# The last 64 rows of w_down on 64 partitions in place of 128, in a decode layer on one core

## The chip, the core and the metric

The kernel runs on one core of one Trainium2 chip. A core has five engines that take instructions in parallel (TensorE or PE, VectorE or DVE, ScalarE or ACT, GpSimd or POOL, and SyncE or SP) and 16 DMA engines. The metric is the device time of one execution in microseconds (us); lower is better.

## The reference

One token goes through one transformer layer: attention with a cached K and V, then a gated feed-forward block. Everything is bf16.

```
h  = x + attention(layernorm(x), k_cache, v_cache) @ wo      # x is 1 x 640; 32 heads, 4096 keys, 128 wide
n  = layernorm(h)
g, u = n @ w_gate, n @ w_up                                  # 640 x 1728 each
h2 = h + (gelu(g) * u) @ w_down                              # 1728 x 640
```

The two caches have 33.6 MB each, wq and wo 5.2 MB each, w_gate, w_up and w_down 2.2 MB each. Each byte is used once.

## The kernel before, in words

**Loads.** SBUF holds three big slots. The K and V caches come in four groups of eight heads, one transfer for each, and pass through the slots in turn; slot 2 also holds wq first and the feed-forward weights at the end. SP issues nearly all transfers on one queue, in the order of the code. A load waits until the last reader of its slot is done. The feed-forward weights wait for the last use of the third K block (`done[("K", 3)]`), and come in this order: the last 64 rows of w_down (80 KB, line 449), w_gate, w_up in two pieces, then the rest of w_down: rows 0 to 1535 in three pieces (line 453: 1280 KB, 480 KB and 160 KB) and rows 1536 to 1663 in two column pieces (line 454: 64 KB and 96 KB).

**Set-up.** GpSimd builds small masks and selection matrices, some in scratch space of slot 2; VectorE reduces some of them. The second K block is loaded over that scratch space, so its load (in line 429) waits for `free2` (line 300), which lists the query projection `qd` and the last readers of the masks. Two of these are for the change: `c_par` (lines 249 and 263) makes `par`, 1 on even partitions in its first column and on odd ones in its second, and `c_sel2` (line 254) makes `sel2`, a 64 x 128 matrix that spreads 64 values over 128 partitions, each to two neighbours.

**Attention.** For each group VectorE multiplies K by the query (line 312), TensorE and VectorE sum the products (lines 29, 320 and 329), ScalarE takes the exponentials, and TensorE multiplies by V (line 355). The output projection with wo follows (lines 397 to 402).

**Feed-forward.** `glu` (line 488) multiplies the normalized h by w_gate and w_up into rows of PSUM; `turn` (line 499) turns each row into 14 columns, so that value f = 128 m + p of the last two blocks, and similar for the others, stands on a partition; the gelu is worked out in a few VectorE and ScalarE steps (lines 525 to 534). The result is `hm`, 128 x 14 in bf16. Column 13 holds the last 64 values, on partitions 0 to 63; its other half is zero.

**The last projection.** `down` (line 536) runs over blocks m of w_down and over four column ranges q (cut at 0, 128, 256, 448 and 640). For each it loads a column of `hm` as weights and streams the block's columns, accumulating in one PSUM row of `ps_d` for each q. Block 13 is special: its 64 rows of 640 were loaded as 128 half rows of 320, two partitions for each row (line 449). So its weights must stand on 128 partitions: `hp` (line 551) spreads column 13 of `hm` with a matmul by `sel2`, and `h2` (line 553) multiplies the result by `par` into `hm2`, whose two columns are for the left and the right halves. Block 13 then has five matmuls, since the range 256 to 448 crosses the middle at 320; it goes first, in line 554. Blocks 0 to 7, 8 to 10, 11 and 12 follow in lines 555 to 560, each behind its own transfer. VectorE and ScalarE copy the four results out (lines 563 and 565), and SP stores them.

Of the kernel before, what the change touches and what calls it, by code (L numbers as in the profile page):

```python
# [5 lines left out]
FP32 = mybir.dt.float32  # L6
BF16 = mybir.dt.bfloat16
ALU = mybir.AluOpType
ACTF = mybir.ActivationFunctionType
AX = mybir.AxisListType  # L10
# [100 lines left out]
def bass_sequential_preLN__gqa_block_cached__glu_gated_geglu__decode_kernel(nc, A_x, A_k_cache, A_v_cache, A_wq, A_wo, B_x, B_w_gate, B_w_up, B_w_down, out):  # L111
    sb = lambda name, shape, dt: nc.alloc_sbuf_tensor(name, shape, dt)
# [32 lines left out]
    e_t = sb("e_t", [128, 14], FP32)  # L145
    gu = sb("gu", [128, 14], FP32)
    hm = sb("hm", [128, 14], BF16)
    hm2 = sb("hm2", [128, 2], BF16)
    sel2 = sb("sel2", [64, 64, 2], BF16)
    par = sb("par", [128, 2], FP32)  # L150
    one_bf = sb("one_bf", [1, 1], BF16)
    one_f = sb("one_f", [128, 1], FP32)
    mean_f = sb("mean_f", [128, 128], FP32)
# [16 lines left out]
    first_t = Cut(slots[2], 5 * 4096)  # L170
    ones_b = first_t.take(128)
    m4_t = first_t.take(128).rearrange("p (a b) -> p a b", a=4)
    hs_t = first_t.take(128).rearrange("p (a b c) -> p a b c", a=8, b=4)
    m8_t = first_t.take(128).rearrange("p (a b) -> p a b", a=8)
    par_t = first_t.take(128).rearrange("p (a b) -> p a b", a=2)
    x_row = first_t.take(D, 1)
    last_t = Cut(slots[1], 0)
    A_hi, A_lo = last_t.take(D), last_t.take(D)
# [10 lines left out]
    ps_d = bank[4][:, 264:456]  # L189
    ps_s = bank[5]  # L190
    ps_z = bank[6]
# [7 lines left out]
    wd_sb = slots[2][:, 10 * DF:10 * DF + 14 * D].rearrange("p (m n) -> p m n", m=14)  # L199

    P = Prog(nc)
    V = lambda fn, *d: P.op("vector", fn, *d)
    A = lambda fn, *d: P.op("scalar", fn, *d)
    T = lambda fn, *d: P.op("tensor", fn, *d)
# [32 lines left out]
    def mask(dst, src, pattern, base, cm, op, *deps):  # L237
        return GP(lambda e: e.affine_select(dst, src, pattern=pattern, compare_op=op, fill=0.0, base=base,
                                            channel_multiplier=cm), *deps)
    c_idb = mask(id_b[:, :], ones_b[:, 0:128], [[1, 128]], 0, -1, ALU.is_equal, c_onesb)  # L240
# [4 lines left out]
    c_m4 = mask(m4_t, ones_b[:, 0:128].rearrange("p (a b) -> p a b", a=4), [[-1, 4], [-4, 32]], 0, 1, ALU.is_equal)  # L245
    c_hs = mask(hs_t, ones_b[:, 0:128].rearrange("p (a b c) -> p a b c", a=8, b=4), [[-4, 8], [-32, 4], [-1, 4]], 0, 1,
                ALU.is_equal)
    c_s4 = mask(sel4[:, :], ones_b[:, 0:4], [[-32, 4]], 0, 1, ALU.is_equal)
    c_par = mask(par_t, ones_b[:, 0:128].rearrange("p (a b) -> p a b", a=2), [[-1, 2], [-2, 64]], 0, 1, ALU.is_equal)
    c_hx = mask(hbx[:, :, :], ones_b[:, 0:32].rearrange("p (a b) -> p a b", a=8), [[-16, 8], [0, 4]], 0, 1, ALU.is_ge)  # L250
    c_hx = mask(hbx[:, :, :], hbx[:, :, :], [[16, 8], [0, 4]], 15, -1, ALU.is_ge, c_hx)
    c_sel = mask(sel[:, :, :], ones_b[0:16, 0:128].rearrange("p (a b) -> p a b", a=16), [[1, 16], [0, 8]], 0, -1, ALU.is_equal)
    c_m8 = mask(m8_t, ones_b[:, 0:128].rearrange("p (a b) -> p a b", a=8), [[-1, 8], [-8, 16]], 0, 1, ALU.is_equal)
    c_sel2 = mask(sel2[:, :, :], ones_b[0:64, 0:128].rearrange("p (a b) -> p a b", a=64), [[1, 64], [0, 2]], 0, -1,
                  ALU.is_equal)

    c_odd = V(lambda e: e.reduce_sum(odd[:, :], hb[:, 8:16].rearrange("p (a b) -> p b a", b=2), axis=AX.X), c_hb)
    c_far = V(lambda e: e.tensor_scalar(far[:, :, :], odd[:, :].unsqueeze(2).to_broadcast([128, 2, 16]), -1e38, 1e38, ALU.mult, ALU.add), c_odd)
    c_m4 = V(lambda e: e.reduce_sum(m4[:, :], m4_t, axis=AX.X), c_m4)
    c_m8 = V(lambda e: e.reduce_sum(m8[:, :], m8_t, axis=AX.X), c_m8)  # L260
    c_hs = V(lambda e: e.reduce_sum(hs[:, 8:16], hs_t.rearrange("p a b c -> p a (b c)"), axis=AX.X), c_hs, c_hz)
    c_o4 = V(lambda e: e.reduce_max(ones4[:, :], sel4[:, :], axis=AX.X), c_s4)
    c_par = V(lambda e: e.reduce_sum(par[:, :], par_t, axis=AX.X), c_par)


    def x_cols(e):
# [30 lines left out]
        return i  # L297
    qd = T(q_proj, xl, d_wq)
    q1 = V(lambda e: e.tensor_copy(qb[:, :, :].rearrange("p g d -> p (g d)"), ps_q[:, :]), qd)  # L299
    free2 = [qd, c_sel2, c_par, c_m4, c_m8, c_hs, c_idb]  # L300

    folds, reds, exps, pbs, pvs, mks, evs, hds, nbs = {}, {}, {}, {}, {}, {}, {}, {}, {}
    z4s, spr, aPs = {}, {}, {}
# [103 lines left out]
    for G in range(NG):  # L407
# [32 lines left out]
        if G == 2:  # L440
# [5 lines left out]
    free = done[("K", 3)]  # L446
    wu_v = B_w_up[:, :].rearrange("(p c) n -> p c n", c=5)
    wd_v = B_w_down[0:1536, :].rearrange("(p r) n -> p r n", r=12)
    d_wd = [P.dma("sync", wd_sb[:, 13, 0:320], B_w_down[1664:1728, :].rearrange("f (s n) -> (f s) n", s=2), free)]
    d_wg = P.dma("sync", wg_sb, B_w_gate[:, :].rearrange("(p c) n -> p c n", c=5))  # L450
    d_wu = [P.dma("sync", wu_sb[:, 0:3, :], wu_v[:, 0:3, :]),
            P.dma("sync", wu_sb[:, 3:5, :], wu_v[:, 3:5, :])]
# [12 lines left out]
    hi = [V(lambda e: e.tensor_copy(A_hi[0:97, 0:320], bank[0][0:97, 0:320]), pr),  # L465
          A(lambda e: e.copy(A_hi[0:97, 320:640], bank[1][0:97, 0:320]), pr)]
    lo = [V(lambda e, t=t: e.tensor_sub(A_lo[0:97, 320 * t:320 * t + 320], bank[t][0:97, 0:320], A_hi[0:97, 320 * t:320 * t + 320]),
            hi[t]) for t in range(2)]
# [65 lines left out]
    g9 = V(lambda e: e.tensor_mul(hm[:, :], gu[:, :], ps_u[:, 0:14]), g6, up)  # L534

    def down(ms, qs=range(4)):
        def fn(e):
            for m in ms:
                for q in qs:
                    lo, hi = CUT[q], CUT[q + 1]  # L540
                    if m < 13:
                        parts = [(hm[:, m:m + 1], lo, hi, 0)]
                    else:
                        parts = [(hm2[:, s:s + 1], max(lo, 320 * s), min(hi, 320 * s + 320), 320 * s) for s in range(2)]
                    for w, a, b, base in parts:
                        if a < b:
                            i = e.matmul(ps_d[32 * q:32 * q + 1, a - lo:b - lo], w, wd_sb[:, m, a - base:b - base],  # L547
                                         start=False, stop=(m == 12), skip_group_check=(m == 13))
            return i
        return fn  # L550
    hp = T(lambda e: e.matmul(ps_z[:, 0:1], sel2[:, :, :].rearrange("p a b -> p (a b)"), hm[0:64, 13:14],
                              start=True, stop=True), g9, c_sel2)
    h2 = V(lambda e: e.tensor_mul(hm2[:, :], par[:, :], ps_z[:, 0:1].to_broadcast([128, 2])), hp)
    T(down([13]), h2, d_wd[0])
    T(down(range(8)), d_wd[1])
    T(down(range(8, 11)), d_wd[2])
    T(down([11]), d_wd[3])
# [40 lines left out]
```

## Time and profile before

| | |
|---|---|
| three runs, median | 202.17 us (201.92 to 202.38) |
| the profiled execution, its own time | 201.75 us |
| its span, first to last instruction | 200.5 us |
| granted TensorE clock, mean | 0.901 |
| PE, busy | 107.0 us (53%), 771 matmuls |
| PE weight loads, busy | 17.3 us (9%), 490 loads |
| DVE, busy | 118.5 us (59%), 160 instructions |
| ACT, busy | 6.7 us (3%) |
| POOL, busy | 4.2 us (2%) |
| DMA | 84.32 MB in 2890 packets, mean 421 GB/s |

The profile is of one execution, whose span starts at its first instruction; all times within it count from there. The page gives the busy time of each engine, then the span in 40 slices of equal length with the busy share of each in tenths, then the DMA queues, then the chain of waits: from the last instruction back to whatever released each step. Groups of instructions carry the line of the kernel, the engine, the operation, and the tiles they write and read. "PEld" is a weight load on TensorE, "SPq" a DMA issue by SP. A wait for several things is put down to the one that came last by the trace.

### The profile page before, as it was taken

How to read it: one execution, taken by the hardware profiler on the slowest of the kernel's cores; microseconds unless marked ns; L12 is line 12 of the kernel's file. 1: busy time of each engine (PE TensorE's matmuls, PEld its weight loads, DVE VectorE, ACT ScalarE, POOL GpSimd, SP SyncE). 2: the span in 40 equal slices, each digit the busy share in tenths (PEclk: the TensorE clock that was granted, in tenths of full speed). 3: DMA queues.
4: the chain of work that ended last, by engine and by line, in shares of the span. 5: the costliest groups of instructions: out<-in, count | busy, mean ns of one | idle time of the engine just before them, and what ended most of it. 6: DMA issues, size and time to landing. Idle time of an engine off the chain costs nothing.

```text
span 200.5 us, 1514 instructions
## 1 busy us (share of the span) xinstructions
PE 107.0 (53%) x771; PEld 17.3 (9%) x490; DVE 118.5 (59%) x160; ACT 6.7 (3%) x18; POOL 4.2 (2%) x19
## 2 busy tenths in 40 slices
PE   0108000586674408476745095855086897475584
PEld 0103000000001100000022000000000020231232
DVE  3300100889975027999750569997879969624331
ACT  2100000000001000000010000000100000100111
POOL 7100000000000000000000000000000000000000
PEclk9999999999996976999978759999859999979758
DMA  9999999999999999999999999999999998999993
GB/s 360 417 466 431 418 418 418 418 418 510 484 445 431 397 418 431 431 418 431 418 418 422 431 484 458 445 431 418 431 418 431 431 431 368 429 425 425 407 413 121
DMA packets 2890, 84.32 MB, mean 421 GB/s; under 512 B 322, under 2 KB 836, under 8 KB 1092
## 3 DMA queue, kind: packets, MB, share of 16 engines
q1 hardware_dynamic: 2882, 84.23, 97.9%
q8 instruction: 5, 0.08, 0.2%
q14 instruction: 1, 0.01, 0.0%
q10 hardware_dynamic: 2, 0.00, 0.0%
HBM read 84.23 MB, written 0.00 MB: 420 GB/s over the span
## 4 chain that ended last, share of the span: by engine, by line
DMA 52%; DVE 30%; PE 15%; SPq 1%; issue 1%; ACT 0%
DMA slot<-in_A_k_cache_dram 39%; DVE slot L312 21%; DMA slot<-in_B_w_down_dram 12%; PE bank L29 9%; DVE sc L329 6%; PE bank L355 4%; SPq L60 1%; DVE mix L343 1%; PE bank L320 1%; PE bank L547 1%; DVE mx L334 0%; ACT p_t L339 0%; DVE mix L361 0%; DVE mxd L335 0%; DVE mxd L337 0%
## 5 line engine op out<-in xcount | busy, mean ns | idle before, releaser
L312 DVE TENSOR_TENSOR slot<-slot,qb 128x4096 bf16<-128x4096 bf16 x32 | 72.6, 2280 | 32.9 <-DMA slot<-in_A_k_cache_dram 32.9
L29 PE MATMUL bank<-slot,id_b 128*128 128x512 bf16 x249 | 66.0, 417 | 27.2 <-DVE slot L312 27.2
L329 DVE TENSOR_REDUCE sc<-bank 128x32 f32<-128x512 f32 x32 | 21.9, 683 | 11.6 <-PE bank L29 11.6
L355 PE MATMUL bank<-slot,mix 128*32 128x512 bf16 x256 | 19.3, 468 | 8.8 <-DVE mix L343 8.8
L320 PE MATMUL bank<-slot,id_b 128*128 128x512 bf16 x7 | 3.4, 483 | 34.2 <-DVE slot L312 34.2
L355 PEld LDWEIGHTS bank<-slot,mix 128*32 128x32 bf16 x256 | 7.8, 115 | 76.5 <-DVE mix L343 42.1
L295 PE MATMUL bank<-slot,xlnM 128*32 128x512 bf16 x40 | 4.5, 631 | 7.1 <-DMA slot<-in_A_wq_dram 7.1
L339 ACT ACTIVATE p_t<-sc,nb 128x256 bf16<-128x256 f32 x4 | 2.0, 508 | 161.0 <-DVE nb L338 161.0
L343 DVE TENSOR_TENSOR mix<-p_t,hbx 128x512 bf16<-128x512 bf16 x16 | 5.7, 420 | 2.7 <-ACT p_t L339 2.7
L299 DVE CAST qb<-bank 128x512 bf16<-128x512 f32 x1 | 0.7, 691 | 10.1 <-PE bank L295 10.1
L494 PE MATMUL bank<-slot,hlnT 128*1 128x512 bf16 (+1 forms) x40 | 4.8, 552 | 2.1 <-DVE hlnT L482 1.5
L361 DVE TENSOR_TENSOR mix<-bank,m 128x512 f32<-128x512 f32 x4 | 2.7, 682 | 4.4 <-PE bank L355 4.4
L268 PE MATMUL bank<-one_bf,slot 1*128 1x1 bf16 x5 | 0.4, 177 | 7.0 <-DMA slot<-in_A_x_dram 7.0
L320 PEld LDWEIGHTS bank<-slot,id_b 128*128 128x128 bf16 x7 | 0.7, 99 | 37.2 <-DVE slot L312 36.8
L369 PEld LDWEIGHTS bank<-po_r,hb 128*16 128x16 f32 x8 | 0.5, 95 | 31.5 <-issue 31.5
L400 PE MATMUL bank<-slot,aP 128*1 128x320 bf16 x32 | 2.5, 298 | 1.0 <-DMA slot<-in_A_wo_dram 1.0
L29 PE MATMUL bank<-slot,aP 128*1 128x320 bf16 x32 | 2.5, 298 | 0.0
L295 PEld LDWEIGHTS bank<-slot,xlnM 128*32 128x32 bf16 x40 | 1.6, 141 | 9.2 <-issue 9.2
L547 PE MATMUL bank<-slot,hm 128*1 128x128 bf16 (+2 forms) x57 | 2.1, 233 | 0.6 <-DMA slot<-in_B_w_down_dram 0.4
L371 PE MATMUL bank<-po_r,hs 128*16 128x128 f32 x8 | 1.5, 274 | 1.0 <-DVE po_r L365 1.0
L563 DVE CAST slot<-bank 1x128 bf16<-1x128 f32 (+1 forms) x2 | 0.6, 316 | 2.3 <-PE bank L547 2.3
L515 PE MATMUL bank<-mix,one_f 128*1 128x128 f32 (+1 forms) x8 | 2.0, 460 | 0.0
(91 smaller groups left out, 40.6 us busy)
## 6 DMA issues: line engine op xcount, KB each, us to landing
slot<-in_A_wq_dram SPq DMA_DIRECT2D x1, 5120.0 KB, 15.4
slot<-in_A_wo_dram SPq DMA_DIRECT2D x2, 2560.0 KB, 15.9
slot<-in_B_w_gate_dram SPq DMA_DIRECT2D x1, 2160.0 KB, 17.4
slot<-in_B_w_up_dram SPq DMA_DIRECT2D x1, 1296.0 KB, 20.1
slot<-in_B_w_down_dram SPq DMA_DIRECT2D x1, 1280.0 KB, 24.3
slot<-in_B_w_up_dram SPq DMA_DIRECT2D x1, 864.0 KB, 21.7
slot<-in_B_w_down_dram SPq DMA_DIRECT2D x1, 480.0 KB, 25.0
slot<-in_B_w_down_dram SPq DMA_DIRECT2D x1, 160.0 KB, 25.0
```

Of the source, the lines that this page charges most:

```text
L29: return e.add_instruction(mybir.InstMatmult(name=nc.get_next_instruction_name(), engine=e.engine, start_tensor_calc=start, stop_tensor_ca ...
L60: ev = self.op(eng, lambda e: e.dma_start(out, in_), *deps, dma=True)
L295: i = e.matmul(ps_q[32 * j:32 * j + 32, :], xlnM[:, 160 * s + 32 * c:160 * s + 32 * c + 32], wq_j[:, c, 2 * j + s, :, :], start=(c == 0 an ...
L312: m = V(lambda e: e.tensor_tensor(out=kt, in0=kt, in1=qb[:, G, :].unsqueeze(1).to_broadcast([128, 32, DH]), op=ALU.mult), landed[("K", G)] ...
L320: i = e.matmul(*args, start=True, stop=False)
L329: reds[(G, c)] = V(lambda e: e.reduce_sum(sc[:, 32 * c:32 * c + 32], ps_f[c % 2][:, :].rearrange("p (g d) -> p g d", d=16), axis=AX.X), fo ...
L343: pbs[(G, n)] = pbs[G] = V(lambda e, lo=lo, hi=hi: e.tensor_tensor(out=p_bd[:, lo:hi, :].rearrange("p c (a r) -> p c a r", a=8), in0=p_t[: ...
L355: i = e.matmul(po[a:a + 32, 0:512], p_bd[:, c, :], vt[:, 4 * c:4 * c + 4, :], start=(c < 4), stop=(c >= 60))
L361: mks[G] = V(lambda e: e.tensor_tensor(out=po_m, in0=po[:, 0:512].rearrange("p (b d) -> p b d", b=4), in1=m4[:, :].unsqueeze(2).to_broadca ...
L400: r = e.matmul(*args, start=start, stop=stop)
L494: i = e.matmul(po[32 * a:32 * a + 1, 512 * k:512 * k + n], hlnT[:, c:c + 1], cols, start=(c == 0), stop=(c == 4))
L547: i = e.matmul(ps_d[32 * q:32 * q + 1, a - lo:b - lo], w, wd_sb[:, m, a - base:b - base], start=False, stop=(m == 12), skip_group_check=(m ...
```

## The change

The last 64 rows of w_down are loaded as 64 whole rows on partitions 0 to 63. Block 13 uses column 13 of `hm` over 64 partitions directly, with four matmuls. The spread, the mask, and the constants for them go; `free2` names two other masks, which stand later in GpSimd's order than those that are left.

```diff
-    hm2 = sb("hm2", [128, 2], BF16)
-    sel2 = sb("sel2", [64, 64, 2], BF16)
-    par = sb("par", [128, 2], FP32)
...
-    par_t = first_t.take(128).rearrange("p (a b) -> p a b", a=2)
...
-    c_par = mask(par_t, ones_b[:, 0:128].rearrange("p (a b) -> p a b", a=2), [[-1, 2], [-2, 64]], 0, 1, ALU.is_equal)
...
-    c_sel2 = mask(sel2[:, :, :], ones_b[0:64, 0:128].rearrange("p (a b) -> p a b", a=64), [[1, 64], [0, 2]], 0, -1,
-                  ALU.is_equal)
...
-    c_par = V(lambda e: e.reduce_sum(par[:, :], par_t, axis=AX.X), c_par)
...
-    free2 = [qd, c_sel2, c_par, c_m4, c_m8, c_hs, c_idb]
+    free2 = [qd, c_m4, c_m8, c_hs, c_idb, c_sel, c_s4]
...
-    d_wd = [P.dma("sync", wd_sb[:, 13, 0:320], B_w_down[1664:1728, :].rearrange("f (s n) -> (f s) n", s=2), free)]
+    d_wd = [P.dma("sync", wd_sb[0:64, 13, :], B_w_down[1664:1728, :], free)]
...
             for m in ms:
+                n = 128 if m < 13 else 64
                 for q in qs:
                     lo, hi = CUT[q], CUT[q + 1]
-                    if m < 13:
-                        parts = [(hm[:, m:m + 1], lo, hi, 0)]
-                    else:
-                        parts = [(hm2[:, s:s + 1], max(lo, 320 * s), min(hi, 320 * s + 320), 320 * s) for s in range(2)]
-                    for w, a, b, base in parts:
-                        if a < b:
-                            i = e.matmul(ps_d[32 * q:32 * q + 1, a - lo:b - lo], w, wd_sb[:, m, a - base:b - base],
-                                         start=False, stop=(m == 12), skip_group_check=(m == 13))
+                    i = e.matmul(ps_d[32 * q:32 * q + 1, 0:hi - lo], hm[0:n, m:m + 1], wd_sb[0:n, m, lo:hi],
+                                 start=False, stop=(m == 12), skip_group_check=(m == 13))
             return i
         return fn
-    hp = T(lambda e: e.matmul(ps_z[:, 0:1], sel2[:, :, :].rearrange("p a b -> p (a b)"), hm[0:64, 13:14],
-                              start=True, stop=True), g9, c_sel2)
-    h2 = V(lambda e: e.tensor_mul(hm2[:, :], par[:, :], ps_z[:, 0:1].to_broadcast([128, 2])), hp)
-    T(down([13]), h2, d_wd[0])
+    T(down([13]), g9, d_wd[0])
```

## The prediction

> **What bounds the kernel now.** I read the page first, from its slices down to its chain, then the windows of the last 20 us, then the timeline of the end, then the DMA issues one by one.
>
> The slices and the queues come first:
>
> ```profile
> DMA  9999999999999999999999999999999998999993
> GB/s 360 417 466 431 418 418 418 418 418 510 484 445 431 397 418 431 431 418 431 418 418 422 431 484 458 445 431 418 431 418 431 431 431 368 429 425 425 407 413 121
> q1 hardware_dynamic: 2882, 84.23, 97.9%
> HBM read 84.23 MB, written 0.00 MB: 420 GB/s over the span
> ```
>
> The row of DMA is at nine tenths or more in 38 of 40 slices, at eight tenths in one, and falls only in the last. The one big queue is busy for 97.9% of the 16 engines' span. VectorE, the next busiest, has 59%. So the kernel lasts as long as its 84.23 MB take, and an edit counts where it changes that stream or what comes after its last byte.
>
> The chain of waits agrees, at its end above all (start, length, what):
>
> ```profile
> 172.63 25.03 DMA slot<-in_B_w_down_dram
> 197.66 0.04 issue
> 197.71 0.42 PE bank L547 x10
> 198.13 0.04 issue
> 198.16 0.77 PE bank L547 x8
> 198.93 0.35 DVE slot L563
> ```
>
> Behind line 547 stand the matmuls of the last projection, the very ones that the change touches, and each batch of them starts after a transfer of w_down. The chain stops at the landing of 197.66, but two later transfers matter more. The issues asked singly give 173.11 + 25.0 = 198.1 us for the 160 KB piece and 177.50 + 21.0 = 198.5 us for the 96 KB piece, the last of all. The timeline puts the last two weight loads of line 547 at 198.56, right behind. So the wait that ends last is for the 96 KB transfer; after it come matmuls, copies to 199.28, the output's issue at 199.34 and its landing at 200.5.
>
> The windows of the end show how the stream runs dry (busy time and count per engine, clock, DMA share, GB/s):
>
> ```profile
> 183.00:195.00 12.00, 8.29 (x98) 3.38 (x82) 5.05 (x19) 1.74 (x5) 0.00 (x0) 0.72 1.00 418
> 195.00:196.00 1.00, 0.52 (x8) 0.34 (x7) 0.19 (x2) 0.17 (x1) 0.00 (x0) 0.94 0.96 377
> 196.00:197.00 1.00, 0.75 (x34) 0.66 (x36) 0.16 (x1) 0.00 (x0) 0.00 (x0) 1.00 0.80 286
> 197.00:197.60 0.60, 0.35 (x16) 0.11 (x4) 0.00 (x0) 0.00 (x0) 0.00 (x0) 1.00 0.35 122
> 197.60:198.10 0.50, 0.39 (x12) 0.18 (x12) 0.00 (x0) 0.00 (x0) 0.00 (x0) 1.00 0.39 109
> 198.10:198.60 0.50, 0.47 (x10) 0.21 (x8) 0.00 (x0) 0.00 (x0) 0.00 (x0) 0.94 0.00 0
> ```
>
> Until 195 all engines work. Then the share falls to 0.80 and to 0.35: about ten of the sixteen are done a microsecond before the rest. So the end belongs to some six late DMA engines. A delay on one of these goes into the time whole; on an early one it is hidden up to about 1 us.
>
> **The change, part by part.** The removed steps stand in the timeline of the end:
>
> ```profile
> 195.77 0.17 DVE L534 TENSOR_TENSOR hm<-gu,bank 128x14 bf16<-128x14 f32 x1 [0.75 <-PE bank L507]
> 195.99 0.09 PEld L551 LDWEIGHTS bank<-hm,sel 64*128 64x128 bf16 x1 [0.42 <-DVE hm L534]
> 196.00 0.17 PE L551 MATMUL bank<-hm,sel 64*128 64x1 bf16 x1 [0.33 <-DVE hm L534]
> 196.21 0.16 DVE L553 TENSOR_TENSOR hm<-par,bank 128x2 bf16<-128x2 f32 x1 [0.27 <-PE bank L551]
> 196.42 0.69 PEld L547 LDWEIGHTS bank<-slot,hm 128*1 128x1 bf16 x37 [0.33 <-DVE hm L553]
> 197.71 0.18 PEld L547 LDWEIGHTS bank<-slot,hm 128*1 128x1 bf16 x12 [0.60 <-DMA slot<-in_B_w_down_dram]
> ```
>
> *The spread and the mask (lines 551 and 553).* They go, and with them the way from 195.99, when TensorE could take hm, to 196.42, when it could take hm2: 0.43 us. Block 13 then has four matmuls in place of five. At 0.69/37 = 19 ns a load that is another 0.02 us. So block 13 is issued by about 195.99 + 4 x 0.02 = 196.07 in place of 196.52. What is late next is the 1280 KB piece of w_down: issued at 172.16, landed 24.3 us later, at 196.5. Before, block 13's five loads ended as it landed; after, TensorE stands idle for 0.4 us and starts blocks 0 to 7 at the same 196.5. Behind these 32 matmuls it idles again, 0.36 us by the timeline, until the next landing. Value: nothing. What hides it are the transfers; with that cover gone it would be worth 0.43 + 0.02 = 0.45 us.
>
> *A matmul over 64 rows in block 13.* The nearest rows are line 551's load and matmul over 64 rows, 92 and 174 ns, beside 82 and 219 ns for line 547. Four of them cost between 0.04 us more and 0.2 us less, all before 196.5. Value: nothing.
>
> *The set-up.* GpSimd loses two masks (about 0.39 and 0.71 us, means of their groups), VectorE one reduction (0.28 us), all over by 5.7 us. VectorE's next work waits for x and starts at 7.39. SP's wait before the second K load did name line 263, the removed reduction, for 4.1 us, but then waited 14.3 us more for the query projection (line 295) and issued at 20.05; that is late next. The two masks now waited for instead end by 4.6 us. Nothing there, and the queue holds K and V transfers meanwhile. x_row and some constants move by a few hundred bytes; I give that nothing.
>
> *The 80 KB transfer.* This is the one edit inside the stream. It is still the first of eight issues behind the third K block, at 170.36, and it costs SP the same one instruction (0.33 us); nothing waits behind it, since 5 MB of w_o are still under way. It landed 12.7 us later, at 183.0, and is wanted at 196. So 13 us cover its own lateness; only what it takes from the transfers queued behind it counts. Before, it took about 0.2 us: w_o's second half landed at 164.1 + 18.8 = 182.9. That agrees with 81,920 B at the stream's 430 GB/s, 0.19 us. After, 64 rows of 1280 B. The nearest row is the 160 KB piece, 128 rows of 1280 B, which landed 0.45 us after the one ahead of it: half of it makes 0.22 us. So +0.02 us. What the trace does not show is a large transfer that lands on 64 partitions only. Bounds: -0.19 us, if the late engines get none of it (their 5120 B at 430/16 = 26.9 GB/s), and +0.57 us, if only four engines carry it (20,480 B each, 0.76 us). I take +0.02, by the 160 KB row, which has the same row length and the same queue.
>
> [...]
>
> **Sum.** The profiled execution took 201.75 us, 200.5 of it span and 1.25 around it. With 0 for the TensorE path, 0 for the set-up and +0.02 for the transfer it would take 201.8. The median of the runs shown is 202.17, 0.42 over it; the difference added to that gives **202.2 us**.
>
> **Rivals.**
>
> [...]
>
> *Slower: few DMA engines carry it.* If the 64 rows are dealt out so that only some engines get any, each of these falls behind and never catches up, because everything behind is dealt evenly. At eight engines that is 10,240 B, +0.19 us; at four +0.57 us, or 202.7; over 0.4 us it takes 15,900 B an engine, so five engines or fewer, and a late one among them. For it: the windows show that engines do not level out. Against it: 64 divides by sixteen as 128 does. [...]
>
> *Faster: TensorE was the later one.* In the profiled execution block 13's loads ended just as the 1280 KB landed. If in other executions the stream is ahead of TensorE to the end, the 0.45 us comes through: 201.7. Against it: behind blocks 0 to 7 TensorE waits 0.36 us again, and then for two more landings, so the stream would have to be about 0.9 us faster at its end.
>
> **How the numbers follow.** The forecast 0.43; half the destinations 0.25; few engines 0.21; TensorE later 0.08; 0.03 for something not thought of, split between the signs. About 0.2% (0.4 us) is what a measurement of this kernel can tell from no change: the three runs span 201.92 to 202.38. The forecast is "same" but for about 0.04 on either side. Of the second case, 0.06 comes out slower by scatter; of the third, 0.18 is slower and 0.03 same; of the fourth, 0.06 is faster and 0.02 same. So faster 0.11, same 0.59, slower 0.30. The range goes from 201.7, where the third rival ends, to 203.0, the four engines' 202.7 and the scatter above it.
>
> **What would show each step.** Lines 551 and 553 gone, the first matmul of line 547 at about 0.2 us behind hm, and then an idle time of some 0.4 us that ends with a landing: right. [...] A transfer of 80 KB whose landing lies more than 0.5 us behind w_o's second half, and a DMA share that falls below 0.9 around 182 to 183.5 or tails off later than 198.1: few engines. A landing no longer ahead of the last loads of line 547: TensorE was the later one. The prediction is wrong if the time moves by over 0.4 us while the 80 KB transfer still takes 0.2 us; then the cause lies in something that I priced at nothing.

## The result, and the profile after

The changed kernel takes 202.51 us (median of 12 runs, 202.34 to 202.82), the kernel before 202.01 us (12 runs, 201.87 to 202.38). The ratio is 1.0023, with a 95% interval of 1.0016 to 1.0031: slower by about half a microsecond, a little over the 0.4 us that I had set as the bound of no change. It lies in the range given (201.7 to 203.0), but 0.3 us over the forecast of 202.2, and the mechanism is not the one that I chose.

The profiled execution took 202.52 us, with a span of 201.3 us. The same rows of its page as shown of before, the slices and the queues:

```profile
DMA  9999999999999999999999999999999999999993
GB/s 350 424 477 417 417 417 417 417 469 482 495 417 417 396 430 430 417 430 417 417 469 459 482 417 417 417 430 430 417 443 417 417 446 394 419 425 373 411 413 114
q1 hardware_dynamic: 2818, 84.23, 97.8%
HBM read 84.23 MB, written 0.00 MB: 419 GB/s over the span
```

The bytes are the same, the packets are 64 fewer, and the queue is as busy as before. It is still the stream that sets the time. One number stands out: slice 37 (181 to 186 us) has 373 GB/s, where the kernel before has 425, at a full row of DMA. The DMA engines are at work there and move less.

The chain of waits of its last part, then the windows of the end:

```profile
173.16 25.27 DMA slot<-in_B_w_down_dram
198.43 0.04 issue
198.47 0.42 PE bank L534 x10
198.89 0.01 issue
198.90 0.50 PE bank L534 x6
```

```profile
196.00:197.00 1.00, 0.44 (x6) 0.34 (x6) 0.22 (x3) 0.39 (x1) 0.00 (x0) 1.00 0.95 351
197.00:197.60 0.60, 0.39 (x18) 0.29 (x22) 0.16 (x1) 0.00 (x0) 0.00 (x0) 1.00 0.64 231
197.60:198.10 0.50, 0.50 (x32) 0.38 (x18) 0.00 (x0) 0.00 (x0) 0.00 (x0) 1.00 0.37 131
198.10:198.60 0.50, 0.25 (x14) 0.13 (x12) 0.00 (x0) 0.00 (x0) 0.00 (x0) 1.00 0.48 139
198.60:199.00 0.40, 0.39 (x16) 0.14 (x8) 0.00 (x0) 0.00 (x0) 0.00 (x0) 1.00 0.08 27
```

The end has its old shape, about 0.7 us later: the share is 0.95 where it was 0.80, and the last bytes move after 198.6 where they had stopped by 198.1. The 96 KB transfer, issued at 174.6, landed 24.7 us later, at 199.3, against 198.5. DMA engines that finish early and those that finish late are both later, so this is not a few of them fallen behind.

Where is it lost? I followed the landings back. The first half of w_o landed 13.0 us after its issue in both kernels. The second half landed 18.8 us after its issue before and 19.3 after. The 80 KB landed at 183.1 before and at 183.9 after. So the loss begins just as the 80 KB transfer, queued behind w_o, is carried. The windows of that stretch show it, first of the kernel before, then of the changed one (busy times and counts, clock, DMA share, GB/s):

```profile
180.00:184.00 4.00, 2.30 (x51) 0.77 (x27) 1.42 (x5) 0.00 (x0) 0.00 (x0) 1.00 0.98 410
```

```profile
180.00:184.00 4.00, 0.75 (x17) 0.29 (x12) 0.66 (x2) 0.00 (x0) 0.00 (x0) 0.75 1.00 351
```

The DMA share is 1.00, so all sixteen DMA engines are at work, but they move 351 GB/s in place of 410. (A packet is counted whole in the window in which it starts, so a share can stand a little over 1.00.) Over 4 us that is 59 x 4 = 236 KB not moved, or 0.55 us of the stream at 430 GB/s. The single packets in the trace's records say who is slow: the 64 packets of 1280 B take 55 ns (the median; the slowest 94), as the 1280 B packets of the 160 KB transfer do. The neighbours take longer: w_gate's packets of 17,280 B, all 644 to 658 ns before, take up to 1020 ns. A single slow packet proves little, since one of 1111 ns also stands in a kernel that loses no time (the compute alone, below). But in the changed kernel 44 of w_gate's 128 packets and 8 of w_o's (765 ns at the median before, up to 1129 here) are lengthened by over 5%, all of them between 180.7 and 184.2 us. Together that is 10.3 us of packet time, or 0.64 us for each of sixteen DMA engines: the size of the loss. Looking at the changed transfer alone, one would find next to nothing: its 64 packets take 3.7 us together, and 3.5 where they cost nothing (every second partition, below).

The profiled executions differ by 0.77 us and the medians by 0.50. A part of the rest is older than the transfer: SP issued w_o at 163.86 in place of 163.68, and the 80 KB at 170.54 in place of 170.36, so this execution was 0.18 us late already before the 80 KB moved.

The timeline of the end shows the removed steps gone:

```profile
196.99 0.17 DVE L526 TENSOR_TENSOR hm<-gu,bank 128x14 bf16<-128x14 f32 x1 [0.75 <-PE bank L499]
197.21 0.77 PEld L534 LDWEIGHTS bank<-slot,hm 64*1 64x1 bf16 x36 [0.41 <-DVE hm L526]
198.47 0.18 PEld L534 LDWEIGHTS bank<-slot,hm 128*1 128x1 bf16 x12 [0.49 <-DMA slot<-in_B_w_down_dram]
198.90 0.47 PEld L534 LDWEIGHTS bank<-slot,hm 128*1 128x1 bf16 x8 [0.25 <-DMA slot<-in_B_w_down_dram]
```

Block 13 starts 0.22 us behind the start of hm's instruction, with nothing between. But hm itself came at 196.99 in place of 195.77, with the TensorE clock at half from 182.0 to 195.7 us in this execution (before: 188.3 to 195.1). The 1280 KB piece landed at 172.7 + 24.6 = 197.3, as block 13's loads ended, so all 36 loads go in one run. TensorE then waits for transfers as before, 0.49 and 0.25 us.

### The profile page after: what moved, and what is told of

Read it like the earlier page. It is cut to its first block, busy times and chain, and to the rows that moved or that the text cites. A ratio compares the mean times of both kernels' runs of the same rounds, so it can differ in the third digit from the quotient of the medians.

```text
span 201.3 us, 1505 instructions
## 1 busy us (share of the span) xinstructions
PE 106.1 (53%) x769; PEld 17.0 (8%) x488; DVE 118.1 (59%) x158; ACT 6.7 (3%) x18; POOL 3.3 (2%) x17
## 3 DMA queue, kind: packets, MB, share of 16 engines
q1 hardware_dynamic: 2818, 84.23, 97.8%
## 4 chain that ended last, share of the span: by engine, by line
DMA 52%; DVE 30%; PE 15%; SPq 1%; issue 1%; ACT 0%
DMA slot<-in_A_k_cache_dram 39%; DVE slot L304 21%; DMA slot<-in_B_w_down_dram 13%; PE bank L29 9%; DVE sc L321 6%; PE bank L347 4%; SPq L60 1%; DVE mix L335 1%; PE bank L312 1%; PE bank L534 0%; DVE mx L326 0%; ACT p_t L331 0%; DVE slot L547 0%; DVE mix L353 0%; DVE mxd L327 0%
## 5 line engine op out<-in xcount | busy, mean ns | idle before, releaser
L29 PE MATMUL bank<-slot,id_b 128*128 128x512 bf16 x249 | 66.8, 420 | 26.5 <-DVE slot L304 26.5
L347 PE MATMUL bank<-slot,mix 128*32 128x512 bf16 x256 | 17.9, 442 | 8.8 <-DVE mix L335 8.8
L312 PE MATMUL bank<-slot,id_b 128*128 128x512 bf16 x7 | 3.4, 483 | 34.8 <-DVE slot L304 34.8
L287 PE MATMUL bank<-slot,xlnM 128*32 128x512 bf16 x40 | 3.6, 535 | 7.1 <-DMA slot<-in_A_wq_dram 7.1
L392 PE MATMUL bank<-slot,aP 128*1 128x320 bf16 x32 | 3.3, 380 | 3.2 <-DMA slot<-in_A_wo_dram 3.2
L457 DVE CAST slot<-bank 97x320 bf16<-97x320 f32 x1 | 0.5, 492 | 5.2 <-PE bank L29 5.2
L29 PE MATMUL bank<-slot,aP 128*1 128x320 bf16 x32 | 3.3, 385 | 0.0
L534 PE MATMUL bank<-slot,hm 128*1 128x128 bf16 (+3 forms) x56 | 2.1, 236 | 0.6 <-DVE hm L526 0.3
## 6 DMA issues: line engine op xcount, KB each, us to landing
slot<-in_B_w_down_dram SPq DMA_DIRECT2D x1, 1280.0 KB, 24.6
```

The lines of the kernel that those rows point to most:

```text
L29: return e.add_instruction(mybir.InstMatmult(name=nc.get_next_instruction_name(), engine=e.engine, start_tensor_calc=start, stop_tensor_ca ...
L287: i = e.matmul(ps_q[32 * j:32 * j + 32, :], xlnM[:, 160 * s + 32 * c:160 * s + 32 * c + 32], wq_j[:, c, 2 * j + s, :, :], start=(c == 0 an ...
L312: i = e.matmul(*args, start=True, stop=False)
L347: i = e.matmul(po[a:a + 32, 0:512], p_bd[:, c, :], vt[:, 4 * c:4 * c + 4, :], start=(c < 4), stop=(c >= 60))
L392: r = e.matmul(*args, start=start, stop=stop)
L534: i = e.matmul(ps_d[32 * q:32 * q + 1, 0:hi - lo], hm[0:n, m:m + 1], wd_sb[0:n, m, lo:hi], start=False, stop=(m == 12), skip_group_check=( ...
```

## The experiments

**Theory P.** The loss comes from the 80 KB transfer, because it lands on 64 partitions: while it is under way, the transfers of all engines are slowed. **Rival S**: it comes from the shorter TensorE path or the set-up. **Rival R**: it is the shape, 64 rows of 1280 B, wherever they land. Every ratio below is to the kernel before, run on the same chip in the same job; the microseconds are differences of medians.

**The transfer alone.** The kernel before with one line changed:

```diff
-    d_wd = [P.dma("sync", wd_sb[:, 13, 0:320], B_w_down[1664:1728, :].rearrange("f (s n) -> (f s) n", s=2), free)]
+    d_wd = [P.dma("sync", wd_sb[0:64, 13, :], B_w_down[1664:1728, :], free)]
```

> The kernel before, with only the 80 KB load changed to 64 whole rows on partitions 0 to 63; the spread, the mask and the set-up stay, and block 13 is summed from halves that do not belong to it. Theory P (the landing on 64 partitions slows the neighbouring transfers): the whole loss, +0.4 to +0.6 us on the kernel before, and w_gate packets of up to 1 us near 181 us in place of 0.64. Rival S (the loss comes from the shorter TensorE path or the set-up, by the clock or by timing): within 0.15 us of before.

Measured: 202.56 us, +0.50; ratio 1.0029 (1.0020 to 1.0038). The window from 180 to 184:

```profile
180.00:184.00 4.00, 0.62 (x16) 0.20 (x8) 0.64 (x2) 0.00 (x0) 0.00 (x0) 0.71 1.01 366
```

A full share and 366 GB/s, as in the changed kernel; 46 of w_gate's packets are lengthened, the longest to 958 ns. The whole loss is in this line.

**The compute alone.** The changed kernel with that line put back:

```diff
-    d_wd = [P.dma("sync", wd_sb[0:64, 13, :], B_w_down[1664:1728, :], free)]
+    d_wd = [P.dma("sync", wd_sb[:, 13, 0:320], B_w_down[1664:1728, :].rearrange("f (s n) -> (f s) n", s=2), free)]
```

> The changed kernel, with only the 80 KB load as before, 128 half rows on 128 partitions; block 13 is summed from halves that do not belong to it. Theory P: within 0.15 us of the kernel before, the landing of w_o's second half near 182.9 us of the span again. Rival S: +0.4 to +0.6 us.

Measured: 202.01 us, -0.05; ratio 0.9996 (0.9987 to 1.0004). The same window has 425 GB/s:

```profile
180.00:184.00 4.00, 2.12 (x39) 0.71 (x23) 1.36 (x5) 0.00 (x0) 0.00 (x0) 0.94 1.01 425
```

Taking away the spread, the mask, the fifth matmul and their set-up is worth nothing that can be measured. Rival S is out on both sides. This trace also shows the idle time that the prediction named: block 13 is loaded 0.23 us behind the start of hm's instruction (195.73), and then the loads of blocks 0 to 7 wait for a landing:

```profile
195.96 0.09 PEld L534 LDWEIGHTS bank<-slot,hm 64*1 64x1 bf16 x4 [0.42 <-DVE hm L526]
196.68 0.59 PEld L534 LDWEIGHTS bank<-slot,hm 128*1 128x1 bf16 x32 [0.64 <-DMA slot<-in_B_w_down_dram]
```

**Every second partition.** The same 64 rows of 1280 B, spread over the memory:

```diff
-    d_wd = [P.dma("sync", wd_sb[:, 13, 0:320], B_w_down[1664:1728, :].rearrange("f (s n) -> (f s) n", s=2), free)]
+    d_wd = [P.dma("sync", wd_sb[0:128:2, 13, :], B_w_down[1664:1728, :], free)]
...
-                        parts = [(hm2[:, s:s + 1], max(lo, 320 * s), min(hi, 320 * s + 320), 320 * s) for s in range(2)]
+                        parts = [(hm2[:, 0:1], lo, hi, 0)]
```

> The kernel before, with the last 64 rows as 64 whole rows of 1280 B on every second partition (0, 2, ... 126); block 13 has four matmuls over 128 partitions by the first column of hm2, which is zero on the odd ones. Theory P, that it matters which partitions are written: 0 to +0.15 us on the kernel before. Rival R, that it is the shape, 64 rows of 1280 B with four for each DMA engine, wherever they land: +0.4 to +0.6 us as in the changed kernel. [...]

Measured: 202.13 us, +0.07; ratio 1.0002 (0.9994 to 1.0011). Its window shows no loss either:

```profile
180.00:184.00 4.00, 1.36 (x25) 0.44 (x16) 0.66 (x2) 0.00 (x0) 0.00 (x0) 0.76 1.04 439
```

The same number of rows, of the same length, costs nothing that can be measured if the rows stand on every second partition, and none of w_gate's packets is longer than 666 ns. Rival R is out.

**The upper half.** The changed kernel with block 13 on partitions 64 to 127; the line that matters:

```diff
-    d_wd = [P.dma("sync", wd_sb[0:64, 13, :], B_w_down[1664:1728, :], free)]
+    d_wd = [P.dma("sync", wd_sb[64:128, 13, :], B_w_down[1664:1728, :], free)]
```

> The changed kernel with everything of block 13 on partitions 64 to 127 in place of 0 to 63. Theory P: the same +0.4 to +0.6 us on the kernel before, since it is half of the partitions again. Rival R: the same. A rival by which only the lower half is crowded (other traffic lands there): within 0.2 us of before.

Measured: 202.51 us, +0.45; ratio 1.0022 (1.0013 to 1.0031). The dip is there too:

```profile
180.00:184.00 4.00, 1.75 (x28) 0.63 (x19) 1.17 (x5) 0.00 (x0) 0.00 (x0) 0.91 1.02 387
```

Either half costs the same when it is used alone: +0.50 us on partitions 0 to 63 and +0.45 on 64 to 127. Nor is the granted TensorE clock of the stretch the cause: it was 0.91 here, with the loss, and 0.76 with every second partition, without it.

**Another place in the queue.** The changed kernel with the 80 KB behind w_up:

```diff
-    d_wd = [P.dma("sync", wd_sb[0:64, 13, :], B_w_down[1664:1728, :], free)]
-    d_wg = P.dma("sync", wg_sb, B_w_gate[:, :].rearrange("(p c) n -> p c n", c=5))
+    d_wg = P.dma("sync", wg_sb, B_w_gate[:, :].rearrange("(p c) n -> p c n", c=5), free)
     d_wu = [P.dma("sync", wu_sb[:, 0:3, :], wu_v[:, 0:3, :]),
             P.dma("sync", wu_sb[:, 3:5, :], wu_v[:, 3:5, :])]
+    d_wd = [P.dma("sync", wd_sb[0:64, 13, :], B_w_down[1664:1728, :])]
```

> The changed kernel with the 80 KB issued behind w_gate and w_up in place of first. If the price is that of the landing on 64 partitions, whoever the neighbours are: +0.4 to +0.6 us on the kernel before again, with the packets of w_up and of the 1280 KB of w_down lengthened in place of w_gate's. A rival by which it comes from the place, first behind w_o and among the 17280 B packets of w_gate: within 0.2 us of before.

Measured: 202.61 us, +0.61; ratio 1.0029 (1.0017 to 1.0040). The dip moves with the transfer. The window from 192 to 194 of this kernel, and of the kernel before:

```profile
192.00:194.00 2.00, 2.00 (x23) 0.69 (x16) 0.73 (x2) 0.00 (x0) 0.00 (x0) 0.58 1.00 347
```

```profile
192.00:194.00 2.00, 2.00 (x25) 0.94 (x21) 0.70 (x4) 0.00 (x0) 0.00 (x0) 0.50 1.04 438
```

Between 180 and 184 it runs at 430 GB/s again. The neighbours are now the 1280 KB of w_down (packets of 10,240 B up to 631 ns; before, 389 at the median and 398 at most), and the price is the same within the intervals.

**Measuring the price by itself.** Seven kernels add a load to the kernel before, behind the first 80 KB, into spare space. The edit, here with 64 partitions, and with another target and source in the others:

```diff
+    spare = slots[2][:, 10 * DF + 14 * D:10 * DF + 18 * D]
+    d_sp = P.dma("sync", spare[0:64, 0:640], B_w_down[1664:1728, :])
...
-    P.op("sync", None, d_out)
+    P.op("sync", None, d_out, d_sp)
```

> The kernel before with a second copy of the 80 KB loaded right behind the first, as 128 half rows on 128 partitions, into spare space that nobody reads. It measures what 80 KB cost in the stream: +0.19 us on the kernel before by the stream's 430 GB/s. All theories say the same; this is the base for the three others.

> As the base, but the second copy as 64 whole rows on partitions 0 to 63. The loss of +0.5 us that the change showed should stand here a second time, beside a first copy that costs nothing: +0.19 + 0.5 = +0.7 us on the kernel before. A rival by which the loss hangs on something else near the 80 KB of the changed kernel (its place as first transfer behind the wait for K): +0.2 us.

> As the base, but the second copy as 32 runs of 2560 B on partitions 0 to 31. If the price goes by the number of partitions (a quarter of them takes four times as long), +0.19 + 1.0 to 1.5 us on the kernel before. [...]

> As the run with 32 runs of 2560 B, but on every fourth partition (0, 4, ... 124). If the number of partitions counts: as the other 32, +0.7 us or more on the kernel before. If what counts is which part of the memory is reached, and every fourth partition reaches all of it: as the base, +0.2 us, with at most 0.15 us more.

> As the runs with a second load of 80 KB, as 16 runs of 5120 B on partitions 0 to 15. 32 partitions cost 0.68 us over the base and 64 cost 0.46. If it went by the number of partitions alone, 16 would go on gently, to about 0.9 us over the base, +1.1 us on the kernel before. [...]

> As the runs with a second load of 80 KB, but in two transfers of 32 whole rows, one to partitions 0 to 31 and one right behind it to 64 to 95. If crowding evens out over the 0.2 us that the pair takes: as the base, +0.2 us on the kernel before. If each transfer crowds its half at once: +0.18 + 0.46 = +0.6 us or more.

> The kernel before with an extra load, as in the runs with a second load, but of 160 KB (128 rows) as 64 runs of 2560 B on partitions 0 to 63. The bytes alone are worth 2 x 0.18 = 0.36 us. If the price of the crowding goes with the bytes: 0.36 + 2 x 0.46 = +1.3 us on the kernel before. If it is a price for each such transfer: 0.36 + 0.46 = +0.8 us.

| added load | median, us | over before | ratio (95% interval) |
|---|---|---|---|
| 80 KB, 128 half rows on 128 partitions | 202.33 | +0.18 | 1.0009 (1.0000 to 1.0018) |
| 80 KB, partitions 0 to 63 | 202.79 | +0.64 | 1.0034 (1.0022 to 1.0047) |
| 80 KB, partitions 0 to 31 | 203.01 | +0.86 | 1.0047 (1.0034 to 1.0060) |
| 80 KB, every fourth partition (32 of them) | 202.31 | +0.16 | 1.0011 (1.0002 to 1.0021) |
| 80 KB, partitions 0 to 15 | 203.10 | +1.10 | 1.0050 (1.0037 to 1.0062) |
| 80 KB, 40 on 0 to 31 and 40 on 64 to 95 | 202.76 | +0.76 | 1.0032 (1.0019 to 1.0044) |
| 160 KB, partitions 0 to 63 | 203.73 | +1.73 | 1.0088 (1.0074 to 1.0102) |

The base costs what the stream's rate says, 0.18 us. On 64 partitions the same bytes cost 0.46 us more, the loss of the change a second time. The two rows with 32 partitions are the clearest pair: neighbouring ones cost 0.68 us over the base, every fourth one nothing (-0.02). So in this pair neither the number of partitions nor the length of the runs decides, but which partitions they are. The windows from 180 to 184, first for partitions 0 to 31, then for every fourth:

```profile
180.00:184.00 4.00, 1.53 (x27) 0.54 (x19) 1.45 (x5) 0.00 (x0) 0.00 (x0) 0.95 1.03 378
```

```profile
180.00:184.00 4.00, 2.21 (x40) 0.74 (x24) 1.30 (x5) 0.00 (x0) 0.00 (x0) 0.93 1.03 429
```

Two transfers of 32 rows, one to each half, one behind the other, do not even it out: 0.58 us over the base.

The sizes did not all come out as expected. 160 KB cost 0.36 for their bytes and 1.37 us beyond, three times the price of 80 KB, where I had twice or once: a clear miss. 16 partitions cost 0.92 us over the base, near the 0.9 expected if the price went on gently with the number of partitions. 32 partitions cost 0.68, under the 1.0 to 1.5 of a price that goes by the number of partitions; that is more than the 0.46 of 64, though the intervals of the two overlap. What sets the size is open: from 64 to 32 to 16 partitions the runs grow too (1280, 2560 and 5120 B), and the 160 KB doubled the runs along with the bytes; no run here separates the two. In the kernel with 160 KB the stretch has 325 GB/s, the lowest of all:

```profile
180.00:184.00 4.00, 0.37 (x8) 0.02 (x4) 0.66 (x2) 0.00 (x0) 0.00 (x0) 0.79 1.10 325
```

There the added transfer's own packets grow too: 140 ns at the median, where the same 2560 B take 102 on every fourth partition.

No version beat the kernel before: the compute alone and the strided landing both come out level with it.

## Why the prediction was right or wrong, point by point

*The bound.* Right. The stream sets the time in the changed kernel too (its queue is busy for 97.8%), and the 0.5 us came from inside the stream.

*The spread and the mask, 0.43 + 0.02 us, hidden.* Right: the compute alone gave 0.9996. Even with the transfer late, TensorE waits 0.49 us behind blocks 13 and 0 to 7. The idle time of 0.4 us ahead of blocks 0 to 7 is there in the compute alone (TensorE's matmuls wait 0.47 us); in the profiled execution of the changed kernel hm came so late that it was gone.

*Block 13 over 64 rows, and the set-up.* Priced at nothing; within the same 0.9996.

*The 80 KB transfer, +0.02 us.* This is the step that failed: "I take +0.02, by the 160 KB row, which has the same row length and the same queue." That row shares the length and the queue, but it lands on 128 partitions, and where the rows land is what counts: the transfer alone gave +0.50 us on partitions 0 to 63, and +0.07 on every second partition. The packets themselves did take what the row says, 55 ns at the median; the price fell on the packets beside them, which no row of the trace of before could show. The row was a weak measure besides: it stood at 197.6 to 198.1, where the DMA share was 0.39, not in a full stream. The prediction had named the landing on 64 partitions as the thing not shown, and its bounds (-0.19 to +0.57) held the value, yet it took the end that assumed the unknown away.

*"Half the destinations" (0.25).* No run shows the term behind this chance. What the runs showed in its place: the price hangs on which partitions the rows land on (+0.50 us on 0 to 63, +0.45 on 64 to 127, +0.07 on every second one), and beyond its bytes an added load cost 0.46 us at 80 KB and 1.37 us at 160 KB. What sets the size is open; the trace does not tell where a packet waits, nor which DMA engine carries it.

*The rival "few engines".* Its size (0.19 to 0.57) takes in the 0.50, its mechanism is out. By it the stream would go on at its full rate while a few DMA engines fall behind; in place of that the stretch drops to 351 GB/s, and the neighbours' packets grow. It would also have shown with every second partition, where the same 64 rows of 1280 B are loaded. One of its signs did come, a DMA share that tails off later than 198.1, but because the whole end is later (0.95 in place of 0.80 between 196 and 197).

*The rival "TensorE was the later one".* I gave it 0.08 as a gain that the timed runs might show, and they show none. But the profiled execution with every second partition shows the mechanism, see the last section.

*The signs.* The 96 KB landed at 199.3, not at the 198.5 of before, which the forecast with its +0.02 us would have kept. The 80 KB landed about 0.4 us behind w_o's second half, where it had been 0.2 before: under the 0.5 named for few engines. The last sign, a move of over 0.4 us with the 80 KB transfer itself as short as before, came nearest: its packets kept 55 ns, though not its landing, and the cause lay in what it does to its neighbours, which the sum had at nothing. (It was also called the first of eight issues; there are nine, and nothing hangs on that.)

*The range and the chances.* 202.51 is within 201.7 to 203.0, by the width of the range and not by the sum, which had +0.02 for the step that cost 0.50. "Same" had 0.59; the measured +0.50 us is just on the slower side of 0.4, which had 0.30. Had "half the destinations" carried the measured price, nearly all of its 0.25 would have counted as slower.

## What to carry to other kernels

Where a DMA stream is the bound, as here with its queue busy for 97.9%, ask of a small transfer where it lands, and do not price it by its own bytes alone: here an added 80 KB on 64 or 32 neighbouring partitions cost 0.46 and 0.68 us beyond their bytes and on every fourth partition nothing (-0.02), and the kernel's own 80 KB on every second partition +0.07, which can't be told from nothing. Look for such a loss in the GB/s of the stretch at a full DMA share and in the summed packet times of the neighbours; the transfer's own 80 KB kept 55 ns a packet at the median. And when two rows of a trace compete to price an unknown, ask which feature of the new operation neither of them has.

## What the runs showed of the hardware that I had not expected

The granted TensorE clock differs between executions of nearly the same program (0.819 to 0.901 over the profiled ones), and in one of them it handed the end to TensorE. In the kernel with every second partition the 1280 KB landed 23.9 us after its issue (24.3 before) and the 480 and 160 KB 24.6 after theirs (25.0 before), but the clock was at 0.50 to the end. Its timeline, and its window of the end:

```profile
197.05 2.02 PEld L547 LDWEIGHTS bank<-slot,hm 128*1 128x1 bf16 x56 [0.33 <-DVE hm L553]
```

```profile
197.00:199.40 2.40, 2.35 (x56) 1.85 (x56) 0.05 (x1) 0.02 (x1) 0.00 (x0) 0.50 0.17 54
```

All 56 loads run without a wait for a transfer, at 2.02/56 = 36 ns each in place of 19, and the span is 201.2 us where the kernel before had 200.5. So the 0.9 us that I had counted between the stream and TensorE is not there in this execution. The runs of this kernel take 201.85 to 202.65 us; that the clock makes this spread is not shown, since only one execution of it was profiled.
